# Identity products ahead of the first transposes, a new order of the first steps on every engine, and one block of last products moved from step 21 to step 22

## The chip, the cores and the metric

The kernel runs on one core of a Trainium2 chip. The time is the device time of one execution in microseconds (us), and the number that counts is the median over executions. The engines are TensorE (PE; its weight loads are listed as PEld), VectorE (DVE), ScalarE (ACT), GpSimd (POOL) and SyncE (SP), which here only issues DMAs.

## What is computed

An mLSTM cell over 4 batches, 8 heads, 768 positions and head size 40, followed by a feed-forward network with a multiplied pair of up-projections. All in float32:

```python
for t in range(S):
    m_new = np.maximum(f_gate[:, :, t] + m, i_gate[:, :, t])
    f_stab = np.exp(f_gate[:, :, t] + m - m_new)
    i_stab = np.exp(i_gate[:, :, t] - m_new)
    m = m_new
    C = f_stab[:, :, None, None] * C + i_stab[:, :, None, None] * np.einsum('bhd,bhe->bhde', vt, kt)
    n = f_stab[:, :, None] * n + i_stab[:, :, None] * kt
    h_tilde = np.einsum('bhde,bhe->bhd', C, qt)
    nq = np.einsum('bhd,bhd->bh', n, qt)[:, :, None]
    denom = np.maximum(np.abs(nq), 1.0)
    y[:, :, t] = 1.0 / (1.0 + np.exp(-o_gate[:, :, t])) * h_tilde / denom
x = y.transpose(0, 2, 1, 3).reshape(B * S, H * D)      # 3072 x 320
out = ((x @ w1) * (x @ w2) @ w3) @ w_out               # w1, w2 320x1024, w3 1024x1024, w_out 1024x320
```

## The kernel before, in words

The recurrence is cut into chunks of 64 positions. Two chunks of one batch make a **unit** of 128 positions and 8 heads, 24 units in all; unit n is batch n mod 4, so a batch comes back every fourth unit, with its state carried from one to the next. The gates of all units are worked out once at the start, by scans on DVE (L546-560).

The main loop (L741) runs 32 steps. In step s, TensorE does for unit s the products of q and k (`ss`) and the state's new part (`pc`), and for unit s-1 the products with the values (`ph`) and with the state (`pi`); all of these sit in two PSUM tiles named `cell` (two banks each). From `pi` and `ph` VectorE makes h, the denominator and y of unit s-1 (`outputs`, L403). Around these lie:

- `turn(n)` (L302): transposes of k and q of a unit on TensorE (`pt`), copied to SBUF by ACT as kT and qT. From unit 10 on DVE does it (L308).
- `rows_of_u`, `weights`, `masks` (L284-300): a DVE transpose, eight exponentials on ACT and two masks on POOL, which give the decay weights `pw` of a unit; L383 multiplies `ss` by them, and `ph` of the next step reads the result.
- `weighted` (L318): values times their weights, `vw`, on POOL, read by `pc`. `decayed` (L324) is the old state times its decay, on POOL; L390, L392 and L398 put the new part in, on DVE.
- `out_gate` (L260): the output gate's tanh on ACT, read by L427 on the way to y.
- `twice` (POOL, L460) and `x_trans` (L462): y of a unit, transposed on TensorE (`px`) and copied by ACT into xT, the input of the network.
- `fetch`, `scale_next`, `convert` (L202-242): a piece of the weights comes by DMA as 64-bit words (`raw`, and in the beginning in space lent by w3o and wo), is scaled in two ACT operations (L182, L186; for the first two pieces the second is DVE's L184), and is put together on DVE (L190, L191). The pieces 0 and 1 are w1's first half, 2 and 3 w2's, 4 the remainder rows `wr`; 5 to 9 are the same of the second half.
- `up` and `up_rest` (L598, L611): one up-projection block, 16 products of 128x256 into `pa` and `pb`, then 16 quarter products with `wr`, then ACT's and DVE's product `ab`. Later, w3 and w_out are multiplied into one matrix, w3o (`w3_mm`, `fold`).
- From step 19 on, `up_by_seven` (L648) does the up-projections with seven block products for eight; its sums on DVE are L664, L666 and L691, and the token sums L646. Its partial products share the `cell` tiles with the recurrence, so `ss` of a step waits for L664.
- `ffn_out` (L713): a down-projection block, 8 products of 128x320 with w3o (`po`, or in steps with `up_by_seven` in `cell`), copied by ACT and sent out. There are 24 blocks; `n_down` (L732) says how many in each step.

TensorE's instructions keep the order of the program text (`in_order`). The other engines keep it too, up to step 31, by `keep_order` (L532). DMAs of loads are all issued by SP in the text's order, so the order of the text is the order of every queue. `n_cvt` and `n_fetch` (L735, L736) say how many weight pieces are converted and fetched in each of the first steps.

In step 2 the first up-projection runs inside the step, by a function `between` (L801) which `quarter_work` (L329) calls between y of unit 1 and `ss` of unit 2. It holds the rest of y for unit 0 and 1 (x_trans), the transposes of unit 2, three conversions, the first block of products, and unit 3's weights.

Of the kernel before, what the change touches and what calls it, by code (L numbers as in the profile page):

```python
# [16 lines left out]
def kernel(  # L17
# [75 lines left out]

    def transpose(out, in_, n=P):
        in_order(nc.tensor.transpose(out, in_, ident[0:n, 0:n]))  # L95

    halves = [slice(0, L), slice(L, P)]
    heads = [slice(0, D), slice(DP, DP + D)]
# [125 lines left out]
    def scale_next(early=False):  # L224
        scaled.append(pend.pop(0))
        scale(scaled[-1][1], early)
# [102 lines left out]
    def quarter_work(s, rest, between):  # L329
# [36 lines left out]
        if n < NU:  # L366
            c, b = divmod(n, B)
            kt, vw = kbuf[n % NB], vw_t.pop(n)
            ends = range(2 if c < NT2 - 1 else 1)
            first, second, after = state[b]  # L370
            before_t[n] = first, second
            state[b] = after, second, first
            kT, qT, pw = kT_t.pop(n), qT_t[n], u_t[n]
            for p in range(NP):
                for hip, x in quarters:
                    mm(ss[halves[x], hip, p, :], kT[heads[hip], p, halves[x]], qT[heads[hip], p, halves[x]])
            for p in range(NP):
                for x, e in quarters:
                    if x in ends:
                        mm(pc[halves[e], x, p, :], kt[halves[x], 2 * p + e, :], vw[halves[x], 2 * p + e, :])  # L380
        if n < NU:
            pv = pw.rearrange("p (n two) t -> p two n t", two=2)
            first_read = nc.vector.tensor_tensor(out=pv, in0=ss, in1=pv, op=OP.mult)  # L383
        with tc.issue_after(first_read.ins) if first_read else nullcontext():
            if den:
                den()
            if n < NU:

                if c:
                    nc.vector.tensor_tensor(out=second, in0=pc[:, 0], in1=second, op=OP.add)  # L390
                else:
                    nc.vector.tensor_copy(out=second, in_=pc[:, 0])  # L392
                if len(ends) > 1:
                    decayed(after, second, n, 1)
            if den:
                den()
            if n < NU and len(ends) > 1:
                nc.vector.tensor_tensor(out=after, in0=pc[:, 1], in1=after, op=OP.add)  # L398
            if den:
                done = den()  # L400
        return done if den else first_read

    def outputs(n, pi, ph):  # L403
        c, b = divmod(n, B)
# [54 lines left out]
    def twice(n):  # L459
        nc.gpsimd.tensor_copy(out=y_t[n][:, DM:DM + REM], in_=y_t[n][:, KF * P:DM])  # L460
# [100 lines left out]
    def gate_cols(src, dst, copy):  # L561
# [3 lines left out]
        for c in range(GC // 2):  # L565
            copy(out=dst.rearrange("p (g c) r -> p c g r", g=GR)[:, c], in_=pg[:, c])

    turn(0)
    gate_cols(a, aT, nc.scalar.copy)
    nc.scalar.activation(out=dec, in_=U3[:, :, L - 1], func=AF.Exp)  # L570
# [13 lines left out]
    for x in range(2):  # L584
        mm(pd[halves[x]], odd[:, x].to_broadcast([RG, L]), pick.rearrange("p j g c -> p (j g c)"))
    cols_of_u()
    nc.scalar.copy(out=decay.rearrange("p j c -> p (j c)"), in_=pd)
    rows_of_u(1)
    nc.scalar.activation(out=g, in_=U, func=AF.Exp)
    scale_next(True)  # L590
    convert()

    ffn = ctx.enter_context(tc.tile_pool(name="ffn", bufs=2))
# [147 lines left out]
    for s in range(len(n_up)):  # L741
# [2 lines left out]
        if N_U <= s + 3 < NU:  # L744
            load_u(s + 3)
        if s < 3:
            if s == 2:
                for _ in range(3):
                    fetch(*todo.pop(0))
            load(s + 2, slice(0, 2))  # L750
            if s == 1:
                load_o(2)
            if s == 2:
                for _ in range(2):
                    fetch(*todo.pop(0))
                fetched = 10
            load(s + 2, slice(2, 3))
            if s:
                load_o(s + 2)
        elif s + 2 < NU:  # L760
            load(s + 2)
            load_o(s + 2)
# [24 lines left out]
            seven[0]()  # L787
        now = [ups.pop(0) for _ in range(n_up[s])]
        open_ups = [up(*x) for x in now] if s != 2 else []
        if s == 3:  # L790
            turn(3)
        def rest():
            for x in open_ups:
                up_rest(*x)
            if seven:
                seven[2]()
            if s == 3:
                for _ in range(2):
                    convert()

        def between():  # L801
            twice(1)
            weighted(2)
            rows_of_u(3)
            for _ in range(3):
                scale_next()
            for n in range(2):
                x_trans(n)
            for _ in range(3):
                convert()  # L810
            turn(2)
            block = up(*now[0])
            weighted(3)
            weights(3)
            masks(3)
            out_gate(2)
            convert()
            up_rest(*block)

        gated = None  # L820
        if s <= NU:
            gated = quarter_work(s, rest, between if s == 2 else None)
        else:
            rest()
        with tc.issue_after(gated.ins) if gated else nullcontext():
            if seven:
                seven[3]()
            if NY <= s - 2 < NU:
                x_turn(s - 2)
            for n in () if s == 1 else (s + 2,) if s < B else (s + 2, s + 3) if s == B else (s + 3,):  # L830
                if n < N_U:
                    rows_of_u(n)
            if N_DVE <= s + 1 < NU:
                gated = turn(s + 1)
            if s - 2 in range(4 * GT - 1, NU, GT):
                token_sums((s - 2) // GT)
        if s == 0:
            weighted(1)
            weights(1)
            masks(1)  # L840
            gate_cols(g, gT, nc.scalar.copy)
        if s == NU:
            cell_psum.close()
            banks.extend([ps_m] * 3 + [ctx.enter_context(tc.tile_pool(name="ps_x", bufs=4, space=bass.MemoryType.PSUM))] * 4)
        if s in (2, 3):
            turned, converted = 2, converted + (4 if s == 2 else 2)
        if s + 1 < N_DVE:
            if s not in (1, 2):
                turn(s + 1)
            while turned < min(s - 1, NY):  # L850
                x_trans(turned)
                turned += 1
        if s < NU:
            if 0 < s < NU - 1 and s != 2:
                if s != 1:
                    weighted(s + 1)
                weights(s + 1)
                masks(s + 1)
            if s != 2:
                out_gate(s)  # L860
        if s in (16, 17):
            weight_sums(s - 16)
# [48 lines left out]
```

## Time and profile before

| what | before |
| --- | --- |
| median of 13 executions | 445.5 us (443.89 to 500.5) |
| the profiled execution: its time | 447.8 us |
| its span in the profile | 446.1 us |
| PE busy | 423.3 us (95% of the span), 5207 products |
| PE weight loads busy | 335.1 us (75%) |
| DVE / ACT / POOL busy | 308.1 / 151.4 / 93.5 us |
| DMA traffic | 51.14 MB, 115 GB/s over the span |
| chain of work that ended last | 75% PE, 6% DVE, 5% DMA, 5% SP's queue |

How to read the profile: times are from the start of the span; each row of the timeline has start, duration, engine, line, operation, output<-inputs, shape, and in brackets the engine's idle time before it with what ended it. The row PEclk of the slices, and the clock column of a table of windows, is the share of full TensorE clock that was granted; where no event was recorded it reads 1.00. The profiled execution took 2.3 us more than the median of the runs.

### The profile page before, as it was taken

The numbers are of one execution on the slowest core, as the hardware profiler recorded it, in microseconds if no ns is written. First come the engines' busy times: TensorE is split into PE (matmuls) and PEld (weight loads), VectorE is DVE, ScalarE is ACT, GpSimd is POOL, SyncE is SP. The second block draws the span as 40 slices with busy tenths as digits, with TensorE's granted clock in tenths as the row PEclk, the third lists the DMA queues.
The fourth block names the chain that finished last, engine by engine and source line by source line (L and its number), as shares of the span: only waits on it lengthen the run. The fifth ranks groups of instructions, "written<-read, shape, count | busy, mean of one in ns | idle before, by whom it ended". The sixth has DMA issues, their size and how long they took to land.

```text
span 446.1 us, 12679 instructions
## 1 busy us (share of the span) xinstructions
PE 423.3 (95%) x5207; PEld 335.1 (75%) x5207; DVE 308.1 (69%) x633; ACT 151.4 (34%) x409; POOL 93.5 (21%) x163
## 2 busy tenths in 40 slices
PE   4969999999999998999999999999699999999996
PEld 3858878787778877778777777778578777777774
DVE  6576887778947977857566869677979776444800
ACT  4865765558451553232132321204111111101110
POOL 4430352223302320311347604202200000000000
PEclk9969999999999999899999999999799999999999
DMA  8999976798985697763616746673111110000001
GB/s 184 216 185 203 208 126 124 171 202 180 193 189 155 121 192 161 149 121 71 137 46 152 163 115 126 135 136 103 25 38 36 38 46 15 16 15 16 1 31 44
DMA packets 135210, 51.14 MB, mean 115 GB/s; under 512 B 109360, under 2 KB 126960, under 8 KB 135152
## 3 DMA queue, kind: packets, MB, share of 16 engines
q1 hardware_dynamic: 131552, 46.29, 51.1%
q10 hardware_dynamic: 3600, 4.03, 2.6%
q8 instruction: 41, 0.67, 0.7%
q14 instruction: 17, 0.14, 0.1%
HBM read 44.50 MB, written 5.80 MB: 113 GB/s over the span
## 4 chain that ended last, share of the span: by engine, by line
PE 75%; DVE 6%; issue 5%; DMA 5%; SPq 5%; ACT 2%; POOL 1%; DVEq 0%; POOLq 0%
PE cell L92 18%; PE pa L92 16%; PE po L92 14%; PE pb L92 10%; PE wp L92 8%; PE p L92 5%; SPq L139 1%; PE pt L95 1%; SPq L175 1%; DVE w3T L646 1%; PE px L95 1%; DMA raw<-in_moe_w_dram 1%; SPq L130 1%; DMA out_dram<-o_sb 1%; DMA kbuf<-in_k_dram 1%
## 5 line engine op out<-in xcount | busy, mean ns | idle before, releaser
L92 PE MATMUL po<-w3o,ab 128*128 128x320 f32 x256 | 70.6, 433 | 0.0
L92 PE MATMUL pa<-xT,w 128*128 128x256 f32 x240 | 62.6, 392 | 1.6 <-ACT xT L470 1.6
L92 PEld LDWEIGHTS po<-w3o,ab 128*128 128x128 f32 x256 | 48.4, 190 | 19.7 <-issue 0.4
L326 POOL TENSOR_TENSOR state<-state,decay 128x164 f32<-128x164 f32 x40 | 19.7, 492 | 172.8 <-DVE state L390 112.2
L92 PEld LDWEIGHTS pa<-xT,w 128*128 128x128 f32 x240 | 45.9, 196 | 9.5 <-ACT xT L470 2.1
L294 ACT ACTIVATE pw<-pw,aT 128x64 f32<-128x64 f32 x184 | 46.4, 339 | 2.9 <-ACT o_sb L721 1.4
L299 POOL TENSOR_SCALAR_AFFINE_SELECT pw<-pw 64x512 f32<-64x512 f32 x48 | 38.7, 807 | 37.2 <-ACT pw L294 35.6
L92 PE MATMUL pb<-xT,w 128*128 128x256 f32 x192 | 45.4, 379 | 0.0
L92 PEld LDWEIGHTS pb<-xT,w 128*128 128x128 f32 x192 | 36.5, 190 | 5.0
L92 PE MATMUL wp<-wo,w3T 128*128 128x320 f32 x128 | 36.9, 443 | 0.3 <-DVE ab L619 0.3
L92 PE MATMUL pa<-xT,wr 64*64 64x256 f32 x384 | 37.0, 386 | 0.0
L92 PE MATMUL pb<-xT,wr 64*64 64x256 f32 x384 | 36.4, 380 | 0.0
L619 DVE TENSOR_TENSOR ab<-pb,a_sb 128x512 f32<-128x512 f32 x24 | 16.4, 688 | 28.8 <-ACT a_sb L618 28.7
L666 DVE SCALAR_TENSOR_TENSOR a_sb<-pa,wo 128x512 f32<-128x512 f32 x12 | 8.3, 691 | 40.0 <-PE pa L92 40.0
L618 ACT ACTIVATE a_sb<-pa 128x512 f32<-128x512 f32 x24 | 14.3, 598 | 63.5 <-PE pb L92 63.5
L92 PE MATMUL cell<-w3o,ab 128*128 128x320 f32 x128 | 35.3, 432 | 0.0
L92 PEld LDWEIGHTS wp<-wo,w3T 128*128 128x128 f32 x128 | 24.5, 196 | 10.1 <-issue 0.8
L721 ACT COPY o_sb<-po 128x320 f32<-128x320 f32 x16 | 6.8, 426 | 74.4 <-PE po L92 74.4
L92 PEld LDWEIGHTS cell<-w3o,ab 128*128 128x128 f32 x128 | 24.3, 190 | 9.6
L92 PEld LDWEIGHTS pa<-xT,wr 64*64 64x64 f32 x384 | 18.9, 132 | 14.8 <-issue 8.3
L414 DVE TENSOR_TENSOR h<-cell,h 64x164 f32<-64x164 f32 x88 | 28.7, 326 | 1.6
L92 PEld LDWEIGHTS pb<-xT,wr 64*64 64x64 f32 x384 | 20.1, 133 | 3.0
(139 smaller groups left out, 730.1 us busy)
## 6 DMA issues: line engine op xcount, KB each, us to landing
raw<-in_moe_w_dram SPq DMA_DIRECT2D x64, 128.0 KB, 3.4
kbuf<-in_k_dram SPq DMA_DIRECT2D x24, 160.0 KB, 4.3
vbuf<-in_v_dram SPq DMA_DIRECT2D x24, 160.0 KB, 4.7
o_in<-in_o_gate_dram SPq DMA_DIRECT2D x24, 160.0 KB, 4.8
out_dram<-o_sb ACTq DMA_DIRECT2D x24, 160.0 KB, 1.9
pw<-U_d SPq DMA_DIRECT2D x28, 128.0 KB, 3.4
raw<-in_moe_w_dram SPq DMA_DIRECT2D x5, 512.0 KB, 6.1
raw<-in_moe_w_out_dram SPq DMA_DIRECT2D x8, 320.0 KB, 3.7
```

Of the source, the lines that this page charges most:

```text
L92: in_order(nc.tensor.matmul(out, lhsT=lhsT, rhs=rhs, start=start, stop=stop))
L95: in_order(nc.tensor.transpose(out, in_, ident[0:n, 0:n]))
L130: nc.sync.dma_start(out=dst, in_=rows(src, n))
L139: nc.sync.dma_start(out=dst[p0:p0 + 32, c0:c0 + NP * RAW].rearrange("r (p e) -> r p e", p=NP), in_=of.rearrange("p (r f) d -> r p (f d)", ...
L294: nc.scalar.activation(out=pw[:, h, :], in_=src[:, h, :], func=AF.Exp, bias=aT[:, c, b * H + h:b * H + h + 1])
L299: nc.gpsimd.affine_select(out=pw[r], in_=pw[r], compare_op=OP.is_ge, fill=0.0, base=0, pattern=[[0, H], [1, L]], channel_multiplier=-1)
L326: nc.gpsimd.tensor_tensor(out=new, in0=old, op=OP.mult, in1=decay[:, b * NP:(b + 1) * NP, 2 * c + x:2 * c + x + 1] .to_broadcast([P, NP, D1]))
L414: nc.vector.tensor_tensor(out=part, in0=ph[x][halves[e]], in1=part, op=OP.add)
L618: nc.scalar.mul(out=a_sb, in_=pa, mul=UP ** -2)
L619: nc.vector.tensor_tensor(out=ab_t[gr][j][:, fs[0]:fs[-1] + 1, t0:t0 + a_sb.shape[-1]], in0=pb, in1=a_sb, op=OP.mult)
L666: nc.vector.scalar_tensor_tensor(out=out, in0=p, scalar=UP ** -2, in1=q, op0=OP.mult, op1=OP.add)
L721: nc.scalar.copy(out=o_sb, in_=po)
```

## The change

A function `warm(n)` multiplies the identity by itself n times into a PSUM tile that nobody reads. It is called with 8 ahead of the first transposes and with 4 between the `x_trans` of unit 0 and that of unit 1. In the beginning, the scaling of the second weight piece and unit 1's row transpose go ahead of the decay copy. In step 0, `weights` and `masks` of unit 1 go ahead of its `weighted`, and unit 2's row transpose leaves the step. The decay and state sum of unit 1 are put off into `between`. In step 1 two weight pieces are scaled on ACT, and three more pieces are fetched: two ahead of unit 3's k and q, one ahead of its values; in step 2 two pieces come ahead of unit 4's k and q. `between` is written anew: the products of the up block come ahead of unit 2's transposes, w2's two conversions ahead of unit 2's row transpose. In steps 3, 4 and 5 the transposes of the step's own unit follow the up block's products, and in step 3 two conversions move from ahead of y to behind L383 (`late`). Of the last products, step 21 does one block in place of two and step 22 one in place of none.

```diff
+    def warm(n):
+        bank = mps([P, P], "fill")
+        for _ in range(n):
+            mm(bank, ident, ident)
+
@@ quarter_work(s, rest, between, late)
-                if len(ends) > 1:
+                if n == 1:
+                    put_off.append((after, second, pc))
+                elif len(ends) > 1:
                     decayed(after, second, n, 1)
+            if late:
+                late()
             if den:
                 den()
-            if n < NU and len(ends) > 1:
+            if 1 != n < NU and len(ends) > 1:
                 nc.vector.tensor_tensor(out=after, in0=pc[:, 1], in1=after, op=OP.add)
@@ the beginning
+    warm(8)
     turn(0)
...
     cols_of_u()
+    scale_next(True)
+    rows_of_u(1)
     nc.scalar.copy(out=decay.rearrange("p j c -> p (j c)"), in_=pd)
-    rows_of_u(1)
     nc.scalar.activation(out=g, in_=U, func=AF.Exp)
-    scale_next(True)
     convert()
@@ the steps
-    n_down = [0] * 16 + [2] * 6 + [0] + [1] * 7 + [0, 5]
+    n_down = [0] * 16 + [2] * 5 + [1] * 9 + [0, 5]
-    n_cvt = [0, 0, 2, 0, 1, 2, 3, 3, 3] + [2] * 6
-    n_fetch = [5, 5, 10]
+    n_cvt = [0, 0, 3, 0, 1, 2, 3, 3, 3] + [2] * 6
+    n_fetch = [0, 0, 10]
...
         if s < 3:
-            if s == 2:
-                for _ in range(3):
-                    fetch(*todo.pop(0))
+            for _ in range((0, 2, 2)[s]):
+                fetch(*todo.pop(0))
             load(s + 2, slice(0, 2))
             if s == 1:
-                load_o(2)
+                fetch(*todo.pop(0))
             if s == 2:
-                for _ in range(2):
-                    fetch(*todo.pop(0))
+                load_o(3)
                 fetched = 10
             load(s + 2, slice(2, 3))
             if s:
-                load_o(s + 2)
+                load_o(2 * s)
...
-        if s == 3:
-            turn(3)
+        if s in (3, 4, 5):
+            turn(s)
         def rest():
...
-            if s == 3:
-                for _ in range(2):
-                    convert()
+            if s in (3, 4):
+                out_gate(s - 1)
 
         def between():
             twice(1)
+            x_trans(0)
+            warm(4)
+            x_trans(1)
+            scale_next()
+            convert()
+            convert()
+            rows_of_u(2)
+            convert()
+            rows_of_u(3)
+            weights(2)
+            after, second, pc = put_off.pop()
+            decayed(after, second, 1, 1)
+            nc.vector.tensor_tensor(out=after, in0=pc[:, 1], in1=after, op=OP.add)
             weighted(2)
-            rows_of_u(3)
-            for _ in range(3):
-                scale_next()
-            for n in range(2):
-                x_trans(n)
-            for _ in range(3):
-                convert()
+            masks(2)
+            block = up(*now[0])
             turn(2)
-            block = up(*now[0])
-            weighted(3)
-            weights(3)
-            masks(3)
-            out_gate(2)
+            up_rest(*block)
+            scale_next()
+
+        def late():
             convert()
-            up_rest(*block)
+            convert()
@@ the end of a step
-            for n in () if s == 1 else (s + 2,) if s < B else (s + 2, s + 3) if s == B else (s + 3,):
+            for n in () if s < 2 else (s + 2,) if s < B else (s + 2, s + 3) if s == B else (s + 3,):
...
         if s == 0:
-            weighted(1)
             weights(1)
             masks(1)
+            weighted(1)
...
-            if s not in (1, 2):
+            if s not in (1, 2, 3, 4):
                 turn(s + 1)
...
-            if 0 < s < NU - 1 and s != 2:
-                if s != 1:
+            if s == 1:
+                scale_next()
+                scale_next()
+            if 1 < s < NU - 1:
+                if s != 2:
                     weighted(s + 1)
                 weights(s + 1)
                 masks(s + 1)
-            if s != 2:
+                if s == 2:
+                    weighted(3)
+            if s not in (2, 3):
                 out_gate(s)
```

More of the change, by code (lines that the diff above doesn't have):

```diff
@@ L327, in decayed, with quarter_work @@
                                 .to_broadcast([P, NP, D1]))
-    def quarter_work(s, rest, between):
+    def quarter_work(s, rest, between, late):
         rest()
@@ L401, in quarter_work @@
         return done if den else first_read
+    put_off = []
     def outputs(n, pi, ph):
@@ L796, in rest @@
                 seven[2]()
-            if s == 3:
-                for _ in range(2):
-                    convert()
+            if s in (3, 4):
+                out_gate(s - 1)
         def between():
             twice(1)
-            weighted(2)
-            rows_of_u(3)
-            for _ in range(3):
-                scale_next()
-            for n in range(2):
-                x_trans(n)
-            for _ in range(3):
-                convert()
-            turn(2)
-            block = up(*now[0])
-            weighted(3)
-            weights(3)
-            masks(3)
-            out_gate(2)
+            x_trans(0)
[11 more added lines that the diff above has]
+            nc.vector.tensor_tensor(out=after, in0=pc[:, 1], in1=after, op=OP.add)
+            weighted(2)
+            masks(2)
+            block = up(*now[0])
+            turn(2)
+            up_rest(*block)
+            scale_next()
+        def late():
             convert()
-            up_rest(*block)
+            convert()
         gated = None
         if s <= NU:
-            gated = quarter_work(s, rest, between if s == 2 else None)
+            gated = quarter_work(s, rest, between if s == 2 else None, late if s == 3 else None)
         else:
@@ L845 @@
         if s in (2, 3):
-            turned, converted = 2, converted + (4 if s == 2 else 2)
+            turned, converted = 2, converted + (3 if s == 2 else 2)
         if s + 1 < N_DVE:
-            if s not in (1, 2):
+            if s not in (1, 2, 3, 4):
                 turn(s + 1)
```

## The prediction

> **What bounds the kernel now.** I read the page's slices first, then TensorE's waits, then the two places they point to. The slices (11.15 us each):
> ```profile
> PE   4969999999999998999999999999699999999996
> PEclk9969999999999999899999999999799999999999
> ```
> PE is busy 423.3 of 446.1 us, so PE sets the end nearly everywhere, and what is left is idle PE and slow PE. PE is thin in slices 0, 2 and 28 (0-11, 22-33, 312-323 us), and in 2 and 28 the clock is low too. TensorE's waits past 20 us name the same places:
> ```profile
> PE cell L92 <- DVE wo L664: 3.6, 1, 3.6
> PE px L95 <- DVE y L429: 2.5, 1, 2.5
> ```
> The clock changes only at multiples of 3.413 us from 18.29 (25.12, 31.94, 178.72, 182.13, 318.66, 325.49), so I cut windows there (window, length, PE busy and products, clock, DMA share, GB/s):
> ```profile
> 14.88:18.29 3.41, 3.41 (x46) 1.00 1.07 289
> 18.29:21.70 3.41, 2.41 (x126) 1.00 1.27 168
> 21.70:25.12 3.42, 2.10 (x67) 1.00 0.63 98
> 25.12:28.53 3.41, 1.00 (x5) 0.50 1.21 162
> 28.53:31.94 3.41, 3.41 (x13) 0.50 0.97 250
> 175.30:178.72 3.42, 1.90 (x124) 1.00 1.09 176
> 315.25:318.66 3.41, 0.17 (x10) 1.00 0.12 25
> 318.66:322.08 3.42, 3.42 (x52) 0.50 0.00 0
> ```
> The reader is to see that two windows with 1.2 to 1.6 us of idle lost the clock in the next one. The 1.00 before 18.29 is only the absence of a record, as four transposes show, the same operation twice:
> ```profile
> 15.64 1.06 PE L95 MATMUL pt<-ident,kbuf 128*128 128x128 f32 x4
> 39.96 0.60 PE L95 MATMUL pt<-ident,kbuf 128*128 128x128 f32 x4
> ```
> PE runs at half rate until 18.29. Busy time alone does not decide: 11.46-14.88 is wholly busy and stays slow. I count array work instead: each product's share of the 128x128 array times its time at full clock (8 products of 128x256 take 1.73 us, so 0.108 us for a full 128x128 one). By window: 4.64-8.05 0.97, 8.05-11.46 1.00, 11.46-14.88 0.71, 14.88-18.29 1.18 (clock rises), 318.66-322.08 1.17 (does not), 18.29-21.70 0.92 (kept), 175.30-178.72 0.90, 21.70-25.12 0.70, 315.25-318.66 0.08 (all three lost). An estimate from these rows: kept from about 0.91 us of array work per 3.41 us, gained from about 1.18.
>
> The front's rows:
> ```profile
> 23.32 0.82 DVE L429 TENSOR_TENSOR y<-h,o_in 128x320 f32<-128x320 f32 x1
> 24.30 0.25 PE L92 MATMUL cell<-state,qT 40*64 40x41 f32 x1 [1.22 <-issue]
> 27.53 0.87 PE L95 MATMUL px<-ident,y 128*128 128x128 f32 x3 [2.51 <-DVE y L429]
> ```
> and step 22's:
> ```profile
> 303.19 0.69 DVE L666 SCALAR_TENSOR_TENSOR a_sb<-pa,wo 128x512 f32<-128x512 f32 x1 [5.20 <-PE pa L92]
> 318.49 1.03 PE L92 MATMUL cell<-qT,kT 40*64 40x64 f32 x32 [3.60 <-DVE wo L664]
> ```
>
> **The change part by part.**
>
> *Eight identity products first.* The identity is ready at 1.54, the first transpose waits for k until 5.55. Eight at the half-rate spacing of 0.213 us take 1.7 us, to about 3.4: covered with 2 us to spare (uncovered they cost 1.7). Do they release the clock? Their array work is 0.85 us, and no 3.41 us window holds them and more than a little of the transposes 2.1 us later; 1.18 is not reached. [...] by the rows the gain is 0. I take 0.
>
> *Steps 0 and 1.* The second weight's scaling and the row transpose ahead of the decay copy, masks ahead of vw, unit 2's row transpose moved out: ACT has the same four operations before unit 1's eight exponentials (14.82), DVE's L383 moves 0.3 us up, but ph waits behind transposes on PE until 17.48: 0. vw(1) then ends near 19.3 and is read at 19.8: 0, with 0.5 of cover. In step 1 DVE's order up to y(0) loses the state add (L398, 22.37, waits for POOL). From L425's end at 21.83: o_in 0.50 + y 0.50 gives y(0) at 22.9 against 24.14. Unit 1's last product at 24.30 stood with the px wait right behind it and left when y(0) came; it now leaves at 23.1. From h(1) to y(1) the trace has 24.58 to 27.39 = 2.8, so y(1) comes at 25.95, its copy on POOL at 26.2, px(1) ends near 26.55: 1.85 sooner.
>
> *Step 2.* Four identity products (0.43 us) go between px(0) (23.1-23.5) and px(1), where PE waits for y(1) until 26.05: covered. In 21.70-25.12 they raise 0.70 to 1.13: above 0.91, the clock stays. [...] 1.56 us idle was enough at 178.72. [...] by the rows the half-rate cost of 27.53-31.94, 4.4/2 = 2.2 us, goes. I take the rows. Then pa/pb come ahead of unit 2's transposes. pa waits for the xT copy (26.55-27.05): 0.5 us newly bare on PE. pa, pb 27.1-30.6 (2x1.73), pt 0.9, rest 0.85, so ss(2) starts at 32.3 instead of 35.38: 3.1 us sooner. Needed by then: w2's two conversions on DVE (25.95 + 2x1.12 = 28.2, pb at 28.8); wr's scale on ACT after xT (28.4), its conversion after a row transpose (30.0, read at 31.5); qT(2) on ACT behind eight exponentials (32.2). Added wait: ACT's scale of w2's second piece stands ahead of tanh(1), both xT copies and exponentials(2); that piece landed at 19.82, ACT is there at 19.9.
>
> *Queue.* SP sends two 512 KB pieces (landing intervals 2.67 and 2.46 us) ahead of k3 and q3, then one more before v3 and two before k4. Restacking the before intervals in the new order: k3 31.4, q3 32.5, v3 34.9, last wr piece 42.0, k4 42.7, q4 43.2. pt(3) now stands behind pa/pb of step 3 (36.9), pt(4) at 44.2, wr read at 45.1 after conversion (44.5). It fits, by 0.6 to 1 us: 0, but no more than about 3.7 can be won here. Conversions of step 3 (`late`) hold DVE some 1.5 us at wr, yet h(2), which had waited for them (46.42), now goes first: 0. Transposes after the products in steps 3-5, and tanh moved a step: the same PE work in another order, 0 (+-0.5). POOL's and ACT's instructions of steps 0 to 5 are the same ones in another order.
>
> *Last products.* One block of 8 (8x0.269 = 2.15 us) moves from step 21 to 22, which had none. DVE waits 5.20 us for PE in step 21, so its whole run to L664 (303.19 to 318.44, gapless) shifts up 2.15, and step 22's 3.60 us wait falls to 1.45; the block runs inside it. At 21 DVE's adds ended at 298.0, still 3 us before PE needs them: no new wait. Gain 2.15. Array work around a 1.45 us hole is about 1.0-1.2 in most window positions, below 0.91 only in some 0.3 of 3.41 us; so the half-rate 318.66-325.49 (6.83/2 = 3.4 us) goes as well. Between ends 0 and 3.4 I take 3.4 for this execution.
>
> **The sum.** This execution took 447.8 (span 446.1): 447.8 - 3.1 - 2.15 - 3.4 = 439.2. The median is 445.5, 2.3 lower; where the windows fall, I assume, differs from run to run. Averaged over positions, before loses about 1.7 (front) and 2.5 (step 22) to the slow clock, after 1.0 and 0.2: gains 0.9 + 0.7 + 2.15 + 2.3 = 6.1, so 439.4 from the median. I forecast 439.3.
>
> **Rivals.**
> A: the front gives nothing: a window falling in 23.6-27.0 keeps only 0.7 of array work even with the four, and the late k/q/weights hold step 4. Against: the restacked landings. Then only step 22 stays: 445.5 - 4.4 = 441.1.
> B: the front pays, but step 22's hole stays too long for the clock, or DVE does not move up with PE because its transposes wait for loads. Against: L308 at 311.62 reads what landed by 294.1, L456 at 311.12 what landed by 301.84. 445.5 - 1.6 - (0 to 2.15) = 441.8 to 443.9, say 443.
> C, slower: the five weight pieces ahead of q4. In the trace SP once stood 4.56 us on such a piece (31.98). If DMA stands so again, q4 comes after 44.2 and each us past it delays PE one for one, through ACT's scale, which stands ahead of exponentials(4) and kT(4). It eats the gain of 6.1 when q4 passes 50.3, and at 53 gives 448.2. Against: the pieces' landings already contain that stand.
> D: the eight products release the clock: 2.6 sooner in front, of which the landings leave 0.6: 438.7 or, if loads come sooner too, 436.8.
>
> **How the numbers follow.** My forecast 0.60 (437.5-441), A 0.20, B 0.08, C 0.06, D 0.06. The range 436 to 443.3 takes in A, D and part of B. A measurement here tells about 0.5% (2.2 us) from no change: below 443.3 is faster. Faster: 0.60+0.20+0.06+half of B = 0.89, less 0.04 for DVE or ACT orders I cannot see stalling in the trace: 0.85; same 0.08; slower 0.07.
>
> **What would show it.** Right: px(1) waits under 2.2 us and ends near 26.5; clock 1.00 through 25-32 us; ss(2) near 32.3; the clock still rising at 17-19 us; PE's wait on L664 near 1.4 us and no slow clock near 310-325. Wrong: the first transposes at 0.11 us each (D); pt(3) or pt(4) waiting for kbuf or q_all, or pb for a conversion (C); px(1) still late after y (the state add was not what held it); a wait of over 3 us on L664 (B).

## The result and the profile after

The changed kernel takes 437.1 us (median of 11 executions, 435.71 to 441.16), the kernel before, over all its executions, 445.4 us. The ratio is 0.983, 95% interval [0.981, 0.985]: 7.6 us faster by the ratio. The forecast was 439.3 with a range of 436.0 to 443.3. The time lies in the range, 2.2 us below the forecast; several terms of the sum were far off and partly cancelled, so the nearness of the number is in part luck.

The profiled execution took 438.8 us (span 437.1) against 447.8 (span 446.1) before: 9.0 us less in these two. Of the page: busy time by engine, then the slices of TensorE and of its granted clock.
```profile
PE 423.3 (97%) x5231; PEld 335.5 (77%) x5231; DVE 307.7 (70%) x633; ACT 151.3 (35%) x409; POOL 94.5 (22%) x163
PE   7789799999999999999999999999999999999996
PEclk9859899999999999999999999999999999999999
```
PE is busy 423.3 us in both kernels, although 24 records were added. These take 5.7 us (3.78 and 1.91, below) and stand where PE was idle before; the rest of the work takes 5.7 us less, because less of it runs at the slow clock. That lasts until 18.29 us in before (four transposes take 1.06 at 15.64, 0.60 at full clock) and until 7.81 in after (1.11 at 5.33, 0.60 at 13.53); the windows recorded at 0.50 behind that, the run's end aside, come to 17.1 us in both. The thin slice 28 of before is gone. At the front, slices of 10.9 us, slice 2 (22 to 33 us) has only five tenths of the clock, and slice 4 (44 to 55 us) is thin and slow where before it was full.

TensorE's waits after (engine, line, for what: total, times, longest):
```profile
PE pb L92 <- DVE w L196: 2.4, 1, 2.4
PE pa L92 <- ACT xT L481: 2.2, 3, 0.8
...
PE ph L92 <- DVE pw L388: 1.3, 2, 0.9
PE cell L92 <- issue: 0.8, 2, 0.6
PE px L95 <- DVE y L440: 0.5, 1, 0.5
```
The two waits that the forecast pointed at are gone or small: step 22's wait of 3.6 us for the last products' adds (L664) has no successor, and px waits 0.5 instead of 2.5. A new wait stands first: pb of step 4 for a weight's conversion on DVE (L196), which DVE now does behind L388 (`late`):
```profile
47.56 0.73 DVE L196 CUSTOM_DVE_ANT_0 w<-raw,w 128x1024 uint16<-128x1024 uint16 x1
48.34 2.55 PE L92 MATMUL pb<-xT,w 128*128 128x256 f32 x6 [2.36 <-DVE w L196]
```

The first 28 us of TensorE after (`fill` is the tile that `warm` writes):
```profile
1.59 3.78 PE L92 MATMUL fill<-ident 128*128 128x128 f32 x16 [1.59 <-POOL ident masks.py:199]
5.33 1.11 PE L95 MATMUL pt<-ident,kbuf 128*128 128x128 f32 x4
...
13.53 0.60 PE L95 MATMUL pt<-ident,kbuf 128*128 128x128 f32 x4
...
22.60 0.75 PE L92 MATMUL cell<-state,qT 40*64 40x41 f32 x17 [0.25 <-issue]
23.28 0.90 PE L95 MATMUL px<-ident,y 128*128 128x128 f32 x3
23.98 1.91 PE L92 MATMUL fill<-ident 128*128 128x128 f32 x8
26.34 0.87 PE L95 MATMUL px<-ident,y 128*128 128x128 f32 x3 [0.45 <-DVE y L440]
27.79 3.78 PE L92 MATMUL pa<-xT,w 128*128 128x256 f32 x8 [0.57 <-ACT xT L481]
```
Eight products of fp32 are sixteen records here: `warm(8)` takes 3.78 us and ends as k's first transpose may start. The four transposes of unit 1 take 0.60 us at 13.53 where they took 1.06 at 15.64: the clock was up already. At 26.34 three records of px take 0.87 (0.55 at full clock, in before at 24.47) and at 27.79 eight records of pa take 3.78 (1.99 at full clock, at 36.17): the clock was lost again in between. Windows along the clock's edges (window, length, busy PE, PEld, DVE, ACT, POOL with counts, clock, DMA share, GB/s):
```profile
7.81:11.23 3.42, 2.82 (x60) 2.10 (x59) 2.60 (x6) 3.26 (x14) 0.94 (x3) 1.00 1.23 246
11.23:14.64 3.41, 3.14 (x95) 2.61 (x90) 2.41 (x4) 3.23 (x14) 2.07 (x3) 1.00 1.18 230
14.64:18.05 3.41, 2.33 (x100) 2.07 (x100) 1.39 (x5) 2.41 (x9) 2.46 (x4) 1.00 0.98 272
18.05:21.47 3.42, 2.54 (x60) 2.39 (x62) 2.73 (x8) 2.32 (x5) 0.00 (x0) 0.50 1.23 185
...
28.29:31.71 3.42, 3.42 (x9) 2.70 (x8) 2.87 (x5) 2.60 (x10) 0.17 (x1) 0.50 1.18 231
...
45.36:48.77 3.41, 1.05 (x5) 0.60 (x5) 3.23 (x9) 1.91 (x9) 1.60 (x2) 1.00 0.75 128
48.77:52.19 3.42, 3.42 (x14) 2.87 (x12) 3.25 (x7) 0.36 (x1) 2.71 (x5) 0.50 1.01 317
```
The window 14.64 to 18.05 has 1.1 us of idle and only small products: slow from 18.05 to 31.71. The window 45.36 to 48.77 has 2.4 us of idle, the new wait of pb: slow until 52.19.

Where the 9.0 us lie, read from the starts of each step's first score products (cell<-qT,kT), before and after: step 2 35.38 and 35.14; step 4 50.59 and 54.20; step 9 108.79 and 112.31; step 14 194.96 and 194.09; step 20 286.15 and 284.42; step 23 336.05 and 327.24. So in these two executions the steps up to 8, the front, lose 3.5 us, steps 9 to 19 win 5.3, and steps 20 to 22 win 7.1. The forecast for the same pair was 3.1 won in front, nothing in the middle and 5.55 at step 22.

### The profile page after: what moved, and what is told of

Its sections match the earlier page's. It is cut to its first block, busy times and chain, and to the rows that moved or that the text cites. A ratio compares the mean times of both kernels' runs of the same rounds, so it can differ in the third digit from the quotient of the medians.

```text
span 437.1 us, 12724 instructions
## 1 busy us (share of the span) xinstructions
PE 423.3 (97%) x5231; PEld 335.5 (77%) x5231; DVE 307.7 (70%) x633; ACT 151.3 (35%) x409; POOL 94.5 (22%) x163
## 4 chain that ended last, share of the span: by engine, by line
PE 55%; issue 23%; POOL 8%; DVE 5%; DMA 4%; SPq 3%; ACT 2%; POOLq 0%; DVEq 0%; ACTq 0%
PE cell L92 17%; PE pa L92 12%; PE po L92 10%; PE pb L92 8%; PE p L92 5%; POOL pw L304 3%; DMA raw<-in_moe_w_dram 2%; POOL vw L326 2%; POOL state L331 1%; POOL raw L651 1%; PE pt L95 1%; DMA vbuf<-in_v_dram 1%; SPq L144 1%; DVE w3T L658 1%; ACT pw L299 1%
## 5 line engine op out<-in xcount | busy, mean ns | idle before, releaser
L92 PE MATMUL pb<-xT,w 128*128 128x256 f32 x192 | 46.8, 386 | 2.4 <-DVE w L196 2.4
L92 PE MATMUL wp<-wo,w3T 128*128 128x320 f32 x128 | 35.7, 433 | 0.1
```

The costliest lines, as they stand in the source:

```text
L92: in_order(nc.tensor.matmul(out, lhsT=lhsT, rhs=rhs, start=start, stop=stop))
```

## The experiments

Times are medians, ratios are to the kernel before on the same chip, with 95% intervals. A **hole** is idle time of TensorE that the profile marks `issue`: no wait that it can see ended it. A **slow window** is a stretch of 3.41 us at the clock 0.50.

**e1, the moved block alone** (before with the new list of down blocks):
```diff
-    n_down = [0] * 16 + [2] * 6 + [0] + [1] * 7 + [0, 5]
+    n_down = [0] * 16 + [2] * 5 + [1] * 9 + [0, 5]
```


> The kernel before with only the list of last products changed (one block from step 21 to step 22). Theory 1 (size of the block mis-read): a product of 128x320 is two records in the trace, so the block is 16 x 0.269 = 4.3 us; it fills the whole wait of 3.6 us at step 22 and the slow clock behind it (1.7 to 3.4 us) goes: 438.4 to 440.1, the wait on L664 near 0. Theory 2 (the forecast): the block is 2.15 us, a wait of 1.4 us stays: 439.8 to 440.9. Both: TensorE's holes near 130.6, 178.8 and 268.4 us stay as in the kernel before, because the number of TensorE instructions ahead of them is the same.

Measured: 439.2 us, ratio 0.986 [0.983, 0.990]; 6.1 us by the ratio. TensorE's timeline around step 22:
```profile
312.42 0.66 PE L92 MATMUL cell<-state,qT 40*64 40x41 f32 x32
312.89 0.67 PE L92 MATMUL cell<-qT,kT 40*64 40x64 f32 x32
```
No idle time is left before the row that waited 3.60 us, and the rows run at full clock. From step 20 to step 23 this execution takes 42.82 us, as after does, where before took 49.90: 7.1 us, the 3.60 of the wait and some 3.4 of slow clock. Of the three holes that both theories left in place, the one near 179 us stayed (1.49), but those near 131 and 268 do not show, with the same number of instructions ahead of them. In after the block itself reads:
```profile
305.89 4.47 PE L92 MATMUL cell<-w3o,ab 128*128 128x320 f32 x16
```
It is 4.5 us of work, not 2.15.

**e2, the fills alone** (before with `warm`, `warm(8)` and `warm(4)`):
```diff
+    warm(8)
     turn(0)
...
-            for n in range(2):
-                x_trans(n)
+            x_trans(0)
+            warm(4)
+            x_trans(1)
```


> The kernel before with only the identity products (8 ahead of the first transposes, 4 between the two px). Theory 1 (instruction blocks): the 12 products are 48 more TensorE instructions; the holes near 130.6, 178.8 and 268.4 us, which all lie at the same place of a 256-instruction block, move away and with them the slow clock after 178.8 (2.6 + 1.7 us); the clock also rises near 8 us and the front gains 0 to 2: 439.5 to 442.5. Theory 2 (the forecast): the first eight do nothing, the four keep the clock: 443.2 to 444.4, holes unchanged.

Measured: 442.9 us, ratio 0.994 [0.992, 0.996]; 2.7 us, between the two expected ranges. In its profile step 2 starts at 30.18, 5.2 us ahead of before, but step 6 at 73.43, 1.7 behind: the waits come back. Two of them are holes, and one is a weight's conversion (1.73 us, pb at 43.88):
```profile
43.88 1.56 PE L92 MATMUL pb<-xT,w 128*128 128x256 f32 x6 [1.73 <-DVE w L196]
...
48.40 0.68 PE L92 MATMUL cell<-vbuf,pw 64*64 64x41 f32 x32 [1.54 <-issue]
...
61.03 0.43 PE L92 MATMUL cell<-vw,kbuf 64*64 64x41 f32 x11 [1.11 <-issue]
```
And yet it ends sooner: from step 13 to step 14 it takes 15.43 us where before takes 18.77. Something at 178 us had gone that no part of the change touches; e9 is about that.

**e3, after without both fills** (`warm(8)` and `warm(4)` taken out):
```diff
-    warm(8)
     turn(0)
...
-            warm(4)
```


> The changed kernel without both groups of identity products (new order and moved block stay). Theory 1 (instruction blocks): the holes near 124, 172 and 262 us come back at the same place of a block, with the slow clock after the second, and the front is at half rate until 17 to 19 us: 439.5 to 442. Theory 2 (the forecast): only the clock in the front is worse, by 0.7 to 2.2: 437.8 to 439.3.

Measured: 444.3 us, ratio 0.997 [0.995, 0.999], above both expected ranges: neither had the order itself as a cost (e5). Order and block together are worth 0.3%, so with that order the fills carry 1.4% of after's 1.7%, more than they are worth in the kernel before (0.6%). Its profile has the clock up for the first time at 37.5, and between steps 13 and 14 it takes 18.79 us, as before does:
```profile
182.12 0.51 PE L92 MATMUL cell<-vw,kbuf 64*64 64x41 f32 x24
184.17 0.46 PE L92 MATMUL cell<-vw,kbuf 64*64 64x41 f32 x8 [1.53 <-issue]
```

**e4, after with the two conversions of step 3 early again** (in `rest`, ahead of h(2), and no `late`):
```diff
+            if s == 3:
+                convert()
+                convert()
...
-            gated = quarter_work(s, rest, between if s == 2 else None, late if s == 3 else None)
+            gated = quarter_work(s, rest, between if s == 2 else None, None)
```


> The changed kernel with the two conversions of step 3 put back ahead of h of unit 2 (in rest, as in the kernel before), and nothing put behind L388. Theory 1 (the put-off conversions cost): pb of step 4 no longer waits 2.4 us for the conversion of w2's second half, and the clock is not lost behind that wait (up to 1.7): 433.5 to 435.5. Theory 2 (the forecast, where the put-off conversions cost 0): 436.8 to 437.4.

Measured: 436.2 us, ratio 0.981 [0.977, 0.984], between the two expected ranges: 0.9 us below after, which the intervals do not tell apart. The wait itself is settled: pb no longer waits and the clock stays up through 45 to 55 us. In its place px of step 4 waits, for y and for its copy, 1.1 us together, and the hole at 25.19 is 2.7 us in this execution:
```profile
PE cell L92 <- issue: 2.7, 1, 2.7
...
PE px L95 <- DVE y L440: 0.8, 2, 0.5
PE px L95 <- POOL y L471: 0.7, 1, 0.7
```
So moving the conversions behind h(2) put a wait of 2.4 us and one slow window (1.7 us) where the forecast had put nothing; the earlier h(2) that it buys saves those waits of 1.1. What that comes to in the median stays within the noise.

**e5, the new order alone** (after with the old list of down blocks and no fills):
```diff
-    warm(8)
...
-    n_down = [0] * 16 + [2] * 5 + [1] * 9 + [0, 5]
+    n_down = [0] * 16 + [2] * 6 + [0] + [1] * 7 + [0, 5]
...
-            warm(4)
```


> The kernel after with the old list of down blocks and with neither fill: the new order and the late conversions alone. Theory 1 (the parts add up: order and block without fills measured 444.3, the block alone 6.8 below its own before): 444.3 + 6.8 = about 451, slower than before by 4 to 6 us, because the new order, without products to hold the clock, leaves ss(2) at the slow clock and makes pb of step 4 wait. Theory 2 (the order is worth the 1 to 2 us that the prediction gave it, and it was the block that lost its gain when the fills went): 444 to 445.

Measured: 449.6 us, ratio 1.010 [1.007, 1.014]. By itself the new order is slower than before, by 4.6 us, as theory 1 has it. Its waits are the old ones and the new one together:
```profile
PE cell L92 <- DVE wo L675: 3.6, 1, 3.6
PE cell L92 <- issue: 3.0, 2, 2.1
PE pb L92 <- DVE w L196: 2.4, 1, 2.4
PE px L95 <- DVE y L440: 2.3, 1, 2.3
```
px still waits 2.3 for y(1): taking the state add out of y's way shortened that by 0.2 only. From e5 to e3, which adds the block, it is 1.3%, as in e1: the block adds up with the order.

**e6, after with the first fill only** (`warm(4)` taken out):
```diff
-            warm(4)
```


> The kernel after without warm(4) between the px of units 0 and 1; warm(8) stays. Theory 1 (what the fills give comes from the first: it stands in a wait that is 3.8 us long, releases the clock ahead of ss(0) in some executions, and its 32 instructions move the block boundaries): 437 to 438.5. Theory 2 (the second fill carries it, as the array work that brings the clock back ahead of pa and pb of unit 0): 442.5 to 444.3. The two together (each a part): 439.5 to 441.

Measured: 438.7 us, ratio 0.986 [0.983, 0.990], between theory 1 and the mixture of both. The first fill carries most of the gain (0.997 without either, 0.986 with it); what the second adds, 0.3%, is within the intervals, though px waits 2.2 again and the clock in this execution comes back only at 33.7.

**e8, transposes in place of the fills' products** (the same records and instructions):
```diff
-        for _ in range(n):
-            mm(bank, ident, ident)
+        for _ in range(2 * n):
+            transpose(bank, ident)
```


> The kernel after with each product of a fill replaced by two transposes of the identity: the same number of records and TensorE instructions, the same columns, the same places. Theory 1 ([...] what is left of the fills is their instruction count): the clock is not released by 7.8 in the profile, ss(0) starts at 13.3 or later, 440 to 443. Theory 2 (the clock counts the array's columns whatever the product is): as after, 436.5 to 438.

Measured: 438.7 us, ratio 0.985 [0.981, 0.989], not to be told from after. The clock comes up at 7.69, as in after at 7.81, out of windows that hold nothing but transposes of fp32 (the fill's, then pt and pg); the two pg take 0.44 at 7.49, and 0.39 at 9.61, where before has 0.53 and 0.58:
```profile
1.60 3.68 PE L95 MATMUL fill<-ident 128*128 128x128 f32 x16 [1.60 <-POOL ident masks.py:199]
5.56 1.12 PE L95 MATMUL pt<-ident,kbuf 128*128 128x128 f32 x4 [0.28 <-DMA kbuf<-in_k_dram]
...
13.29 0.60 PE L95 MATMUL pt<-ident,kbuf 128*128 128x128 f32 x4
```
So transposes of fp32 brought the clock up here as the products of after do. Theory 1 thus fell for the clock; the time lies between the two ranges. The trace lists these transposes as MATMUL with the identity, like the products.

**e9, the instructions with a quarter of the array work** (before with twelve products of 32 columns ahead of the first transposes):
```diff
+    def warm(n):
+        bank = mps([P, P], "fill")
+        for _ in range(n):
+            mm(bank[:, 0:32], ident, ident[:, 0:32])
...
+    warm(8)
+    warm(4)
     turn(0)
```


> The kernel before with twelve narrow products (the identity by 32 of its columns) ahead of the first transposes: as many TensorE instructions as both fills have (48), a quarter of their array work, all of it before k lands. Theory 1 (holes of kind issue stand where a block of 256 instructions ends, and 48 more instructions move them): the hole of 1.56 us at 178.76 and the slow window after it (1.7 us of work lost) are gone from the profile, other holes appear or go; 442 to 444. Theory 2 (such holes do not depend on the count of instructions): the holes stay where they are in the program, 445 to 446.

Measured: 442.3 us, ratio 0.994 [0.992, 0.996], the same as e2 with four times the columns. In the kernel before, the fills' whole gain is had by adding 48 instructions, with a quarter of the columns, to TensorE's stream. The place that shows it, first before, then e9:
```profile
176.69 0.51 PE L92 MATMUL cell<-vw,kbuf 64*64 64x41 f32 x24
178.76 0.45 PE L92 MATMUL cell<-vw,kbuf 64*64 64x41 f32 x8 [1.56 <-issue]
179.14 0.90 PE L95 MATMUL px<-ident,y 128*128 128x128 f32 x3
```
```profile
176.54 0.63 PE L92 MATMUL cell<-vw,kbuf 64*64 64x41 f32 x32
177.10 0.55 PE L95 MATMUL px<-ident,y 128*128 128x128 f32 x3
```
The same 32 products stop for 1.56 us after the 24th in one kernel and run through in the other; behind the stop px takes 0.90 in place of 0.55, at the slow clock. Between steps 13 and 14 that is 18.77 us against 15.43. At step 13 the two executions are 0.1 us apart. This hole, between steps 13 and 14, stands in every profile without fills (178.76 in before, 179.07 in e1, 184.17 in e3, 183.77 in e5). After, e4, e9 and e12, with fills, do not have it. The holes at 130.61 and 268.36 are gone in e9 too, but they are also missing in e1, e3 and e5; that the added instructions removed them is not shown.

**e10, after with narrow fills** (32 columns in place of 128, the same instructions):
```diff
-            mm(bank, ident, ident)
+            mm(bank[:, 0:32], ident, ident[:, 0:32])
```


> The kernel after, each product of both fills only 32 columns wide in place of 128: the same products, weight loads and TensorE instructions (48), a quarter of the columns. Theory 1 (the fills are worth what their instructions shift: the holes of kind issue at 131, 178 and 268 go): 437 to 439. Theory 2 (they are worth their array work, through the clock): the clock is not released ahead of ss(0) nor held, 441 to 443.5.

Measured: 439.8 us, ratio 0.987 [0.984, 0.991]. Nearer to theory 1, but between the two: from e3 to after the ratios fall by 1.4%, 6.3 us; the instructions with a quarter of the columns bring 4.3 of it, and the other three quarters of the columns 2.0, which the intervals hardly tell from nothing. The clock in its profile is not up before 33.6, as theory 2 said:
```profile
13.38 1.13 PE L92 MATMUL cell<-qT,kT 40*64 40x64 f32 x32
...
15.64 1.06 PE L95 MATMUL pt<-ident,kbuf 128*128 128x128 f32 x4
```
The released clock of after therefore brings ss(0) 1.6 us and step 2 2.1 us forward, and no more.

**e11, after with wide fills** (512 columns: a quarter of the instructions, the same columns):
```diff
-        bank = mps([P, P], "fill")
-        for _ in range(n):
-            mm(bank, ident, ident)
+        bank = mps([P, 4, P], "fill")
+        for _ in range(n // 4):
+            mm(bank, ident, ident.unsqueeze(1).to_broadcast([P, 4, P]))
```


> The kernel after, with products of 512 columns (the identity four times over) in place of four of 128: two and one in place of eight and four. The same columns of array work, 12 TensorE instructions in place of 48. Theory 1 (instructions): the holes near 131, 178 and 268 are those of the kernel without fills, moved by 12 instructions only, with lost clock behind one of them; 440.5 to 444. Theory 2 (array work): as after, 436.5 to 438.5.

Measured: 439.6 us, ratio 0.986 [0.982, 0.989]: 1.2 us above after by the ratios, which the intervals do not tell apart. The median lies between the two theories, but in its profile theory 1 fell: with a shift of 12 instructions the hole near 178 is gone (as are those near 131 and 268). So e11 does not say whether the columns or the few instructions bring its gain. In front it has holes of 0.79 and 0.81 in the products with the state (0.55 and 0.25 in after), and step 2 starts 1.0 us later than in after.

**e12, block ends moved by 96 instructions** (e4 with another first fill):
```diff
-    warm(8)
+    warm(4)
+    pad(28)
...
+    def pad(n):
+        bank = mps([P, P], "fill")
+        for _ in range(n):
+            mm(bank[0:32, 0:32], ident[:, 0:32], ident[:, 0:32])
```


> The kernel after with the two conversions of step 3 early (as in e4) and with the first fill of four full products and 28 small ones (32 by 32), which is 96 TensorE instructions more. Theory 1 (blocks of 256): the block ends that fell into the products with the state in steps 0 and 1 (count 195 of 256) fall 96 instructions earlier in the program, on the waits for pw (count 99 and 101), and hide there: no hole of kind issue between 15 and 27, about 434 to 436, unless the later block ends fall badly. Theory 2 (holes come wherever the stream is dense, not by the count): a hole of 0.5 to 2.7 stays in the products with the state; 436 to 437.5.

Measured: 440.1 us, ratio 0.987 [0.983, 0.990]: no gain, but by the ratios 2.7 us lost against e4. The hole moved to where the count puts it, 48 records (96 instructions) ahead of e4's at 25.19 and just ahead of the wait for pw, and did not hide there:
```profile
18.23 0.67 PE L92 MATMUL cell<-vw,kbuf 64*64 64x41 f32 x31 [0.92 <-POOL vw L331]
21.15 0.19 PE L92 MATMUL cell<-vw,kbuf 64*64 64x41 f32 x1 [2.26 <-issue]
22.20 1.83 PE L92 MATMUL ph<-vbuf,pw 64*64 64x41 f32 x30 [0.85 <-DVE pw L393]
```
The thirty-second product comes 2.26 us late. DVE's L393, which makes pw out of the products of q and k in the same tile `cell`, starts only behind it (21.45): 0.85 of wait follows the 2.26. A second hole of 1.71 came at 75.14, with a slow window behind it. Where a hole falls can be moved by counting; that it then costs less was wrong.

**e13, the change without its new order** (e2 with the moved block):
```diff
-    n_down = [0] * 16 + [2] * 6 + [0] + [1] * 7 + [0, 5]
+    n_down = [0] * 16 + [2] * 5 + [1] * 9 + [0, 5]
```


> The kernel before with both fills and the moved down block, that is, the change without its new order and without late. Theory 1 (the parts add up, order costs 4 by itself): 445.4 - 6.2 - 2.7 = about 436.5, no slower than after, so that the new order is worth nothing even beside the fills. Theory 2 (the order and the fills need each other: the fills hold the clock only where the order puts the products): 438.5 to 439.5, as the block alone or the order's absence would leave it.

Measured: 436.1 us, ratio 0.979 [0.976, 0.982], the lowest, with e4, and, as theory 1 has it, no slower than after. The new order on all engines, the largest part of the diff, brings nothing beside the fills and the block: it costs 0.4% by the ratios, at the edge of the intervals, although holes take 4.9 us in e13's profile and 0.8 in after's. e13's waits:
```profile
PE cell L92 <- issue: 4.9, 4, 1.8
PE ph L92 <- DVE pw L388: 2.2, 2, 1.1
...
PE px L95 <- DVE y L434: 0.5, 1, 0.5
```
px waits 0.5 for y(1) here too, without the new order, and 2.2 to 2.3 where the second fill is missing (e3, e5, e6): the four products, 1.91 us in after, stand in that time, and the new order of DVE's adds did not bring y(1) sooner.

The parts together (ratio to before):

| order | block | fills | kernel | ratio |
| --- | --- | --- | --- | --- |
| no | no | no | before | 1 |
| no | yes | no | e1 | 0.986 |
| no | no | yes | e2 | 0.994 |
| yes | no | no | e5 | 1.010 |
| yes | yes | no | e3 | 0.997 |
| no | yes | yes | e13 | 0.979 |
| yes | yes | yes | after | 0.983 |

The block is worth 1.3 to 1.5% wherever it was tried. The fills are worth 0.6 to 0.7% without the new order and 1.4% with it: they pay back most of what the order loses. The order costs 1.0 to 1.1% without them and 0.4% with them.

## Why the prediction was right, and where its steps were not

**The last products: right in place, too small in size.** The step failed at "8x0.269 = 2.15 us": a product of fp32 is two records in this trace, so eight products are sixteen records, 4.3 us at 0.269 and 4.47 measured. The words on the kernel before count both ways: the 16 products of an up block are records, the 8 of a down block are products of the program. The wait of 3.60 is filled whole, not down to 1.45. The slow clock behind it, 3.4, went as forecast. 7.0 in place of 5.55 in this execution; as a median 6.1 (e1) in place of 4.45.

**`warm(8)`: the same slip, and rival D.** "Eight at the half-rate spacing of 0.213 us take 1.7 us" became 3.78: the fill reaches from the identity to k's landing with no cover left, where the forecast had 2 us to spare. Its array work is twice the 0.85 that the forecast held against the 1.18, and the clock came up at 7.81 instead of 18.29: the release of D, to which 0.06 was given. It is worth about 2 us in front (e10), and not in every execution: in e4's profile, with the same fill, the clock came up at 17.3. That the forecast counted transposes as array work fits e8, where they alone brought the clock up at 7.69.

**Steps 0 to 2: wrong.** Of the four products between the two px, "they raise 0.70 to 1.13: above 0.91, the clock stays" failed because the loss came a step earlier: the window that ended at 18.05 held only small products, some 0.75 us of array work by the forecast's own measure, and was followed by slow windows until 31.71, past all of px, the fill and pa. They are eight records too, 0.86 of array work and not 0.43, and even so no slow window from 18.05 to 28.29 brought the clock back. Step 2 started at 35.14 and not 32.3. "Unit 1's last product at 24.30 stood with the px wait right behind it" was a misreading: the 1.22 us ahead of it is a hole, marked `issue` in the row of 24.30, not a wait for y. e5 shows the order without help: 2.08 of hole and 2.28 of wait for y(1). The term "3.1 us sooner" was 0.2. Rival A's outcome, nothing won in front, came about, and more was lost; but the cause was an earlier window and the conversion below, not the window and the landings that A named.

**`late`: wrong.** "h(2), which had waited for them (46.42), now goes first: 0" looked at the work that moves up and not at who waits for the work that moves down. pb of step 4 needs the weight that DVE now converts behind h(2): 2.36 us of wait and 1.7 us of slow clock. e4 removes both. The forecast had named "pb for a conversion" as a sign of C, late landings; here it was not one, for ACT had scaled both pieces by 45.4, and DVE took the first at 47.0, behind h(2).

**Queue order: as forecast.** No transpose of k or q waits for a landing in steps 3 and 4 in after's waits, so the late landings of rival C did not come about.

**Not in the sum at all:** 3.3 us between steps 13 and 14 (hole and slow window), and 1.9 us in the other steps from 9 to 19, most of it at the holes of 130.61 and 268.36. No part of the change is near them. The hole before step 14 is gone where the 24 records of the fills (48 instructions with their weight loads) are added, and e9 does not have it either, with a quarter of the array work. The other two are missing without fills too (e1, e3, e5), so that part may be the execution's and not the change's.

So the front, forecast as a gain of 3.1 in the profiled pair (1.6 in the median), lost 3.5 there; step 22 was under-sized by about 1.7 in the median; and some 5 us of the pair, of which 3.3 go with the added instructions, were not in the forecast at all. The sum came out within 2.2 us of the result because these errors cancelled, which is luck; of the gains forecast, the step-22 term alone was right in kind. (The chances given for faster also add up to 0.90 before the 0.04 is taken off, not 0.89.)

**The clock and the array work.** Counted as the forecast did, each record in the window where it starts, the windows of before and after put the two estimates to the test. For keeping: the least that kept the clock was 0.92 us (before, 18.29 to 21.70), and the losses, the run's end aside, came after 0.90, 0.70 and 0.08 in before and after 0.75 (14.64 to 18.05) and 0.86 (45.36 to 48.77) in after. The estimate of 0.91 thus stood in these two profiles. It does not hold in all: e12 lost the clock after a window with 1.28 (73.2 to 76.6) in which the hole of 1.71 stands, and e5 after one with 1.38 (49.6 to 53.0) and 2.0 us of idle. Idle time does not decide either, since e8 kept the clock over a window with 2.0 us of idle and 1.06 of work (41.8 to 45.2). The estimate of 1.18 for gaining did not stand: in after the clock came up behind a window with 1.25 (4.40 to 7.81) and not behind the one ahead of it, with 1.38 (0.99 to 4.40). What decides a gain stays open.

## What to carry to other kernels

Before a row's time is multiplied by a count, count the records of one operation in the trace: for fp32 products it was two. When work is moved behind other work on an engine, price both sides: what comes sooner and who waits for what comes later. And try a reordering without its padding: here the order by itself cost 4.6 us (e5), the fills gave most of it back, and a version without the order (e13) is no slower.

## What the hardware showed that was not expected

TensorE's holes stand at one place of a count of 256 instructions, and a fetch of instructions precedes each. The profiles of before and of after list these fetches (queue, packets, MB, share):
```profile
q8 instruction: 41, 0.67, 0.7%
```
In the trace each of the 41 is 16,384 bytes, and 10,508 instructions of TensorE in before make 256 a fetch, if this queue is TensorE's, which the next count supports. Past 10 us the profiles of before and after have six holes of 0.25 us or more (24.30, 130.61, 178.76 and 268.36 in before, 16.91 and 22.60 in after). All six begin 193 instructions into a block of 256, counted from the first in order of start. Not every hole does: those at 48.40 in e2 and 48.47 in e13 stand at another place: 288 records, 576 instructions, lie between them and the next holes (61.03 and 60.33), and 576 is no multiple of 256. All six are in products of 64 columns or fewer, where 64 instructions pass in 0.5 us and 256 in some 2 us (175.29 to 176.98 in before). A fetch takes 0.88 to 1.79 us in the two traces, and each of the six holes ends 2.4 to 3.1 us after a fetch began (176.12 to 178.76 in before). In after the fetch at the same place in the order, the 20th, began at 171.63, 7.5 us ahead of that instruction: no hole. Counted from the places of the holes, 193 and every 256 on, each fetch of the two traces begins between 42 instructions ahead of one place and 217 behind it, and the holes stand at the next place. Its lead is thus about the time that TensorE takes for one block: long where the products are wide, some 2 us where they are small. That the holes are waits for these fetches is the author's reading of the counts; the trace marks them `issue` and names no cause. By this reading a shift of 12 or 48 instructions can change a fetch's lead. No run here chose the place of a hole and gained by it; e12 tried and lost. In before the hole of 1.56 us cost about as much again, because the clock was lost with it for one window (0.50 from 178.72 to 182.13).
